# GpSimd splits the row maxima and forms most softmax quotients; the turn stands later

## The chip, the cores and the metric

The kernel runs on one core of one Trainium2 chip. The metric is device microseconds (us) of one execution. The engines are named as in the profile: PE (TensorE, matmuls; PEld are its weight loads), DVE (VectorE), ACT (ScalarE), POOL (GpSimd) and SP (SyncE, which here issues all DMAs). Each engine works through its own instructions in order.

## The reference

Two branches read the same input x of 2048 rows and 512 columns, and a gate mixes them. All data are float32.

```python
g = sigmoid((x * gate_w).sum(-1, keepdims=True))
q, k, v = split(x @ wqkv)                      # 32 heads of 16 columns
scores = q @ k.T * 16 ** -0.5                  # per head
scores = where((i - j >= 0) & (i - j < 256), scores, -1e9)
a = (softmax(scores) @ v) @ wo                 # causal, sliding window of 256
b = gelu(x @ w1 + b1) @ w2 + b2                # 1792 hidden columns
out = g * a + (1 - g) * b
```

## The kernel before, in words

**Precision.** A float32 operand is split into a rounded high part and the rest (type `F32R`), and a dense product is three matmuls (`mm3`, L124 to L129).

**Staging.** A generator (`dense`) yields the dense work: q, k and v for four tiles of 512 rows (PSUM name `qk`, `v`), then eight half MLPs (`u` is x @ w1, `y` is h @ w2), then the output projection (`a`). The attention runs beside it in 128 block steps, 8 head groups of 4 heads times 16 blocks of 128 keys. Each step has four pieces of scores for the maxima (`sm`, `att_max`, L541 on PE, reduced on DVE by L545 into `M`), four pieces of transposed scores (`st`, L585), their exponentials on ACT (L607, into `pt`), and after each fourth block a burst of output matmuls (`att_pvs`, L629, names `pv_sm` and `pv_st`). The maxima run 12 steps ahead of the exponentials (`LEAD`). The span for which there is attention goes from about 120 to 670 us.

**Subtracting the maximum.** The exponential of a transposed score needs the maximum of its query, which lies along the columns there. So the maxima of four blocks (`att_rows`) are split into a high and a low part (`nm`, L557 and L558), turned by a 32 x 32 transpose (L560, `tt`, "the turn"), and written by eight small copies on POOL ("the puts", L567) into the rows of `qs` that stand beside the q stack. The k stack `ks` has constant rows there (`own`, L103), so that the matmul adds the maxima to the scores.

**Cutting the triangles.** A block's exponentials outside the window are set to zero by POOL's `affine_select` (L601), four instructions for a block, and for each fourth block four for either half. The burst `att_pvs` of blocks 1 to 3 of the four bursts in a group pairs the oldest block with the newest, and begins with the newest block's second half; the group's first burst takes the blocks in their order and needs it last.

**Quotients.** Two head groups after two fill a chunk of 128 output columns; the sums of exponentials come out of the same matmuls. After the second group's burst `nd` (sums and weighted values, L650 on ACT, L653 on DVE) is stored, `att_norm` loads the denominators, forms reciprocals (L671), stores them (L674), loads them back spread over rows with the values (`num`, `rb`, L679), multiplies (L683) and stores the chunk (L686). That is done 16 times, for 4 chunks c and 4 row tiles t. The buffers `nd`, `num` and `rb` share one tag of three.

**What sets the order.** Nothing is scheduled by a tool: each engine's order is the order in which the code emits. A clock of planned nanoseconds (`now`) moves with each emitted matmul, and `after(ns, fn)` puts a piece of work on a list that is emitted when the clock passes its due time. So a constant such as `PUT`, or a pair in `DIVS`, says how long after its cause a piece stands in the instruction streams. The five numbers of a row of `DIVS` are the due times of the reciprocal, its store, the loads, the product and the chunk's store; the second row is for the last chunk.

Of the kernel before, what the change touches and what calls it, by code (L numbers as in the profile page):

```python
# [13 lines left out]
ALU = mybir.AluOpType  # L14
# [7 lines left out]
NC = D // 128  # L22
# [10 lines left out]
def gated_mix(ctx: ExitStack, tc: tile.TileContext, x, wqkv, wo, w1, b1, w2, b2, gate_w, out):  # L33
    nc = tc.nc
# [11 lines left out]
    def f32(ap):  # L46
        return ap.bitcast(F32)

    tt = cp.tile([128, 2 * RB, 32], F32, name="tt")
# [28 lines left out]
    nms = cs.tile([128, 2 * RB, 32], F32R, name="nm")  # L78
# [5 lines left out]
    def tables():  # L84

        nc.gpsimd.memset(mask, 0.0)
        for r in (0, 64):
            nc.gpsimd.affine_select(out=mask[r:r + 64, 0:64], in_=mask[r:r + 64, 0:64], pattern=[[1, 64]],
                                    compare_op=ALU.is_ge, fill=NEG, base=-1, channel_multiplier=-1)
            nc.gpsimd.affine_select(out=mask[r:r + 64, 256:320], in_=mask[r:r + 64, 256:320], pattern=[[-1, 64]],  # L90
                                    compare_op=ALU.is_ge, fill=NEG, base=0, channel_multiplier=1)
        nc.gpsimd.memset(cut, 3e38)
        for r in (0, 64):
            for e in (0, 1):
                v = cut[r:r + 64, e]
                nc.gpsimd.affine_select(out=v, in_=v, pattern=[[1 - 2 * e, 64]], compare_op=ALU.is_ge, fill=0.0,
                                        base=-e, channel_multiplier=2 * e - 1)
        nc.gpsimd.memset(nil, 0.0)
        nc.gpsimd.memset(own, 0.0)
        for s in (0, 1):  # L100
            for k in (0, 1):
                v = own[64 * s:64 * s + 4].rearrange("r (p s) -> r s p", s=2)[:, s]
                nc.gpsimd.affine_select(out=v, in_=v, pattern=[[-2, 2]], compare_op=ALU.not_equal,  # L103
                                        fill=1.0, base=-k, channel_multiplier=1)
        nc.gpsimd.memset(f32(nms), 0.0)
        nc.gpsimd.memset(vbuf[:, :, NB * 68:], 0.0)

# [26 lines left out]
    def after(ns, fn, *args):  # L134
        now[1] += 1
        heapq.heappush(todo, (now[0] + ns, now[1], fn, args))
# [414 lines left out]
    def att_rows(g_, rb):  # L551
        need(("v", NT - 2, NB - 1))

        need(*[("max", g_, rb * RB + b, i) for b in range(RB) for i in range(4)])
        m = Ms.pop((g_, rb))
        nm = nms[:, :, 0:4].rearrange("p b (i k) -> p k b i", k=2)
        nc.vector.tensor_scalar(nm[:, 0], m, -1.0, None, op0=ALU.mult)  # L557
        nc.vector.scalar_tensor_tensor(nm[:, 1], m, -1.0, f32(nm[:, 0]), op0=ALU.mult, op1=ALU.subtract)  # L558

        nc.vector.transpose(tt.rearrange("p b c -> p (b c)"), f32(nms).rearrange("p b c -> p (b c)"))  # L560

        def put(i, hb):
            r = 64 * (1 ^ hb ^ i // 2)
            dst = qs[r:r + 4, :, rb * RB * 128:(rb + 1) * RB * 128]
            dst = dst.rearrange("r s (b h i j) -> r s b h i j", b=RB, h=2, i=2)[:, :, :, hb, i % 2]
            src = tt[32 * i:32 * i + 4].rearrange("r (b h) j -> r b h j", h=2)[:, :, hb]
            nc.gpsimd.tensor_copy(dst, src.unsqueeze(1).broadcast_to([4, 2, RB, 32]))  # L567
            if i == 3 and hb:
                done.add(("rows", g_, rb))
        for i in range(4):  # L570
            for hb in range(2):
                after(PUT * (i + 1 + 0.5 * hb), put, i, hb)

    def att_exp(g_, kb, i):

# [87 lines left out]
    def att_norm(t, c):  # L663

        v = ND[t][c].rearrange("g (i r) c -> (g i) r c", r=32)
        den = sb.tile([128, 32], F32, tag="den", bufs=1, name=f"den{t}_{c}")
        nc.sync.dma_start(den, v[:, 16, :].rearrange("i (j c) -> i j c", c=32))
        tiles = []

        def rcp():  # L670
            nc.vector.reciprocal(den, den)  # L671

        def keep():
            nc.sync.dma_start(RD[t][c].rearrange("h (j c) -> (h j) c", c=32), den)  # L674

        def back():
            for name, src in (("num", v[:, 0:16, :]), ("rb", RD[t][c].unsqueeze(1).broadcast_to([8, 16, T]))):
                tiles.append(sb.tile([128, T], F32, tag="tmp", bufs=3, name=f"{name}{t}_{c}"))
                nc.sync.dma_start(tiles[-1], src)  # L679

        def mul():
            num, rb = tiles
            nc.vector.tensor_mul(num, num, rb)  # L683

        def store():
            nc.sync.dma_start(OT[t][c], tiles[0])  # L686
            after(REACH, done.add, ("o", t, c))
        for ns, fn in zip(DIVS[c == NC - 1], (rcp, keep, back, mul, store)):
            after(ns, fn)
# [276 lines left out]
    for u in range(-LEAD, NU):  # L966
        m = u + LEAD
# [51 lines left out]
PUT = 1200  # L1019
# [14 lines left out]
HOLD = 4000.0  # L1034
HOLDQ = 1500.0
HOLDO = 3000.0
DIVS = ((8000, 10000, 16000, 23000, 25000), (4500, 5700, 8500, 17000, 18500))
REST = 1000.0
MXAT = 5500.0
AHEAD = 9e3  # L1040
STEP0 = 2750.0
PVAT = 2
HELD = 2
YAT = 5
YGAP = 2500
# [21 lines left out]
```

## Time and profile before

| | |
|---|---|
| median of 3 runs | 717.82 us (714.51 to 720.12) |
| the profiled execution's own time | 720.44 us |
| its span, first to last instruction | 718.6 us |
| mean granted TensorE clock | 0.994 |
| PE busy | 696.9 us, 97% |
| DVE busy | 514.2 us, 72% |
| ACT busy | 420.0 us, 58% |
| POOL busy | 363.5 us, 51% |
| packets of the DMA queue | 85.9% of 16 engines' span |

A busy time is the sum of an engine's instructions in the one profiled execution. Times in the views count from the start of the span, so they lack the 1.8 us that lie around it. A row of the grouped view reads: line, engine, operation, output and inputs, shape, count, then total busy us and mean ns of one, then how long the engine stood idle just before such instructions and who ended that. A row of the waits reads: who waited for whom, us in total, times, longest. A row of the timeline reads: start, duration, engine, line, operation, count, and in brackets the idle time before it and its releaser. A row of one line's own view gives the shortest, median and longest duration in ns.

### The profile page before, as it was taken

To read this page: it belongs to the slowest core of one execution; us is meant where nothing else is said; L and a number is where in the kernel's file an instruction comes from. 1 tells how busy PE (TensorE), PEld (TensorE's weight loads), DVE (VectorE), ACT (ScalarE), POOL (GpSimd) and SP (SyncE) were. 2 spreads that over 40 slices of the span, in tenths; PEclk is the share of its full clock that TensorE was granted. 3 is DMA by queue.
4 is the path that set the end of the run, shared out by engine and by line. 5 is a ranking of instruction groups with operands and counts; after the bars stand their busy time and mean duration, and the time that the engine had idled before them with its cause. 6 is when DMAs were issued, how large, how long until landed. Compare 5 with 4: busy or idle time off the path is not lost.

```text
span 718.6 us, 17501 instructions
## 1 busy us (share of the span) xinstructions
PE 696.9 (97%) x6129; PEld 599.8 (83%) x6129; DVE 514.2 (72%) x1561; ACT 420.0 (58%) x972; POOL 363.5 (51%) x852
## 2 busy tenths in 40 slices
PE   9999999988999999999999999999999999999998
PEld 7888888776888888888888878888888888868877
DVE  3732425778868977987898789868877986875552
ACT  4434532348546944964696469548845953885451
POOL 4200000548766875786687657757765785620000
PEclk9999999999999999999999999999999999999999
DMA  8989898998998698799776989997799899578573
GB/s 296 355 264 408 286 400 252 286 329 199 276 261 194 149 261 218 192 221 273 187 186 162 243 219 234 236 273 175 187 267 231 211 263 248 137 214 224 191 254 118
DMA packets 179255, 172.09 MB, mean 239 GB/s; under 512 B 56672, under 2 KB 122976, under 8 KB 179168
## 3 DMA queue, kind: packets, MB, share of 16 engines
q1 hardware_dynamic: 179168, 170.97, 85.9%
q8 instruction: 49, 0.80, 0.5%
q14 instruction: 38, 0.31, 0.2%
HBM read 108.53 MB, written 62.39 MB: 238 GB/s over the span
## 4 chain that ended last, share of the span: by engine, by line
PE 76%; DMA 9%; DVE 6%; ACT 6%; issue 1%; SPq 1%; POOL 1%; DVEq 0%; ACTq 0%
PE sm L541 8%; PE st L585 7%; PE pv_sm L629 7%; PE y L127 6%; PE y L129 6%; PE y L128 6%; PE u L127 5%; PE u L129 4%; PE u L128 4%; PE qk L127 3%; PE qk L129 3%; PE qk L128 3%; DMA qd<-SQ 2%; DVE sm L545 2%; DMA raw_w<-in_B_w_dram 2%; PE pv_st L629 2%
## 5 line engine op out<-in xcount | busy, mean ns | idle before, releaser
L545 DVE CUSTOM_DVE_ANT_1 sm<-sm,mask 128x320 f32<-128x320 f32 (+4 forms) x512 | 233.0, 485 | 71.1 <-PE sm L541 66.0
L601 POOL TENSOR_SCALAR_AFFINE_SELECT pt<-pt 64x256 f32<-64x256 f32 (+1 forms) x538 | 215.0, 420 | 102.4 <-ACT pt L607 91.8
L607 ACT ACTIVATE pt<-st 128x320 f32<-128x320 f32 (+4 forms) x512 | 195.4, 422 | 118.2 <-PE st L585 117.4
L541 PE MATMUL sm<-kd,qd 96*128 96x320 f32 (+4 forms) x512 | 148.6, 304 | 8.4 <-DVE M L545 5.1
L585 PE MATMUL st<-qs,ks 128*128 128x320 f32 (+4 forms) x512 | 148.0, 300 | 2.6 <-ACT pt L607 2.5
L567 POOL CAST qs<-tt 4x256 fp32r<-4x256 f32 x256 | 120.2, 470 | 42.7 <-DVE tt L560 31.4
L541 PEld LDWEIGHTS sm<-kd,qd 96*128 96x128 f32 x512 | 97.4, 190 | 28.0 <-DVE M L545 11.7
L585 PEld LDWEIGHTS st<-qs,ks 128*128 128x128 f32 x512 | 98.1, 192 | 14.6 <-ACT pt L607 4.5
L127 PE MATMUL y<-w,h 128*128 128x512 f32 x224 | 85.1, 380 | 0.6 <-DVE sqh L746 0.6
L129 PE MATMUL y<-w,h 128*128 128x512 f32 x224 | 84.9, 379 | 0.0
L128 PE MATMUL y<-w,h 128*128 128x512 f32 x224 | 84.8, 379 | 0.0
L127 PE MATMUL u<-mx,w 128*128 128x512 f32 x196 | 77.4, 395 | 1.2 <-DVE sqh L746 1.2
L129 PE MATMUL u<-mx,w 128*128 128x512 f32 x196 | 74.8, 382 | 0.0
L128 PE MATMUL u<-mx,w 128*128 128x512 f32 x196 | 74.7, 381 | 0.0
L629 PE MATMUL pv_sm<-pt,vbuf 64*32 64x320 f32 (+4 forms) x1408 | 73.2, 346 | 0.2 <-POOL pt L601 0.2
L629 PE MATMUL pv_st<-pt,vbuf 64*32 64x320 f32 (+4 forms) x1408 | 72.9, 346 | 0.0
L545 DVE DVE_READ_ACCUMULATOR2_ANT M<- 128x1 f32 x512 | 71.4, 139 | 0.0
L629 PEld LDWEIGHTS pv_sm<-pt,vbuf 64*32 64x32 f32 x1408 | 49.3, 106 | 20.2 <-issue 2.0
L344 DVE TENSOR_TENSOR qke<-qk,qke 128x512 fp32r<-128x512 f32 x32 | 22.1, 689 | 43.2 <-ACT qke L341 33.9
L341 ACT ACTIVATE qke<-qk 128x512 fp32r<-128x512 f32 x32 | 19.1, 597 | 49.9 <-PE qk L129 34.8
L129 PEld LDWEIGHTS y<-w,h 128*128 128x128 f32 x224 | 42.2, 189 | 6.1
L127 PEld LDWEIGHTS y<-w,h 128*128 128x128 f32 x224 | 42.5, 190 | 3.2 <-DVE sqh L746 0.8
(148 smaller groups left out, 1292.0 us busy)
## 6 DMA issues: line engine op xcount, KB each, us to landing
kd<-SK SPq DMA_DIRECT2D x32, 384.0 KB
qs<-SQ SPq DMA_DIRECT2D x64, 192.0 KB
mx<-XT SPq DMA_DIRECT2D x24, 512.0 KB
SQ<-qke SPq DMA_DIRECT2D x16, 512.0 KB
SK<-qke SPq DMA_DIRECT2D x16, 512.0 KB
ND<-nd SPq DMA_DIRECT2D x32, 256.0 KB
raw_w<-in_B_w_dram SPq DMA_DIRECT2D x28, 256.0 KB
qd<-SQ SPq DMA_DIRECT2D x32, 192.0 KB
```

Source lines behind the costliest of these rows:

```text
L127: nc.tensor.matmul(p, lh, rh, start=first, stop=False)
L128: nc.tensor.matmul(p, lh, rl, start=False, stop=False)
L129: nc.tensor.matmul(p, ll, rh, start=False, stop=last)
L341: nc.scalar.activation(halves(e[:, h]), p, AF.Copy)
L344: nc.vector.tensor_sub(halves(e[:, 1 - h]), p, halves(f32(e[:, h])))
L541: nc.tensor.matmul(v, qd[0:96, n, pr, 128 * j:128 * (j + 1)], two(kd[0:96, n, pr, k1 - w:k1]), start=True, stop=True)
L545: nc.vector.tensor_tensor_reduce(v, v, two(mask[:, 320 - w:320]), 1.0, -3e38, ALU.add, ALU.max, M[:, 2 * (b % RB) + hb, pr:pr + 1])
L567: nc.gpsimd.tensor_copy(dst, src.unsqueeze(1).broadcast_to([4, 2, RB, 32]))
L585: nc.tensor.matmul(pairs(p[:, :w]), ks[:, slot(g_, kb // NB), pr, at:at + 128], two(qs[:, pr, k0:k0 + w]), start=True, stop=True)
L601: nc.gpsimd.affine_select(out=v, in_=v, pattern=[[0, v.shape[1]], [1 - 2 * e, 64]], compare_op=ALU.is_ge, fill=0.0, base=-e, channel_multi ...
L607: nc.scalar.activation(halves(pt[:, hf, pr, :w]), sorted_(p[:, :w]), AF.Exp, scale=SCALE)
L629: nc.tensor.matmul(pv[r // 64][32 * i:32 * i + 32, q - c * T:e - c * T], vts[g_, b // NB][r:r + 64, v:v + 32], rhs(r), start=start, stop=s ...
```

## The change

- The split of the maxima moves from DVE to POOL. POOL copies the maximum into its rounded part and subtracts that; the sign that DVE put on is now in the constant rows of the k stacks, which hold -1 in place of 1.
- The turn on DVE is due 3000 ns after the split (`TURN`) where it followed at once, and the eight puts keep their distance from the turn.
- The product `num * rb` moves from DVE to POOL for the first three chunks (12 of 16); the last chunk's four stay.
- For those twelve the product is due 2000 ns later and the chunk's store 3000 ns later.

```diff
-                                        fill=1.0, base=-k, channel_multiplier=1)
+                                        fill=-1.0, base=-k, channel_multiplier=1)
...
         nm = nms[:, :, 0:4].rearrange("p b (i k) -> p k b i", k=2)
-        nc.vector.tensor_scalar(nm[:, 0], m, -1.0, None, op0=ALU.mult)
-        nc.vector.scalar_tensor_tensor(nm[:, 1], m, -1.0, f32(nm[:, 0]), op0=ALU.mult, op1=ALU.subtract)
-
-        nc.vector.transpose(tt.rearrange("p b c -> p (b c)"), f32(nms).rearrange("p b c -> p (b c)"))
+        nc.gpsimd.tensor_copy(nm[:, 0], m)
+        nc.gpsimd.tensor_sub(nm[:, 1], m, f32(nm[:, 0]))
+
+        def turn():
+            nc.vector.transpose(tt.rearrange("p b c -> p (b c)"), f32(nms).rearrange("p b c -> p (b c)"))
+        after(TURN, turn)
...
-                after(PUT * (i + 1 + 0.5 * hb), put, i, hb)
+                after(TURN + PUT * (i + 1 + 0.5 * hb), put, i, hb)
...
         def mul():
             num, rb = tiles
-            nc.vector.tensor_mul(num, num, rb)
+            (nc.vector if c == NC - 1 else nc.gpsimd).tensor_mul(num, num, rb)
...
-DIVS = ((8000, 10000, 16000, 23000, 25000), (4500, 5700, 8500, 17000, 18500))
+DIVS = ((8000, 10000, 16000, 25000, 28000), (4500, 5700, 8500, 17000, 18500))
...
+TURN = 3000
```

The orders of PE and ACT are the same in both kernels. On SP only the twelve stores of chunks stand later, behind one or two more stores. DVE and POOL change throughout; three places follow, in the rows that the built programs print (line, operation, output and inputs, shape; lines after 560 are one to three higher in the changed kernel).

DVE at the turn for blocks 4 to 7 of the first head group, while the last q and k tiles are made (`sm` is a piece of scores, `M` the maxima, `qke` the split q or k). Before:

```order
L545 ISA sm_8_0_1564,M_8_1561<-sm_8_0_1564,mask 128x320
L557 TENSOR_SCALAR nm<-M_4_1395 128x8x2
L558 SCALAR_TENSOR_TENSOR nm<-M_4_1395,nm 128x8x2
L560 STREAM_TRANSPOSE tt<-nm 128x256
L344 TENSOR_TENSOR qke_3_1575<-qk_3_1538,qke_3_1575 128x512
L545 ISA sm_8_3_1586,M_8_1561<-sm_8_3_1586,mask 128x320
```

Now:

```order
L545 ISA sm_8_0_1564,M_8_1561<-sm_8_0_1564,mask 128x320
L344 TENSOR_TENSOR qke_3_1574<-qk_3_1538,qke_3_1574 128x512
L545 ISA sm_8_3_1585,M_8_1561<-sm_8_3_1585,mask 128x320
L545 ISA sm_8_2_1588,M_8_1561<-sm_8_2_1588,mask 128x320
L545 ISA sm_9_1_1602,M_8_1561<-sm_9_1_1602,mask 128x320
L545 ISA sm_9_0_1604,M_8_1561<-sm_9_0_1604,mask 128x320
L561 STREAM_TRANSPOSE tt<-nm 128x256
```

The split is gone from DVE and the turn stands four maxima further back.

DVE at the product of chunk 1, tile 1, while half an MLP is worked (`u`, `sqh`, `x1h` and `h` are the steps of a GELU, `w` a split weight). Before:

```order
L653 TENSOR_TENSOR nd_3_6000<-nd_3_6000,pv_3_sm 128x512
L545 ISA sm_12_2_6007,M_12_5909<-sm_12_2_6007,mask 128x320
L758 TENSOR_TENSOR h_7_5878<-x1h_7_5878_5885,h_7_5878 128x512
L545 ISA sm_13_1_6032,M_12_5909<-sm_13_1_6032,mask 128x320
L683 TENSOR_TENSOR num_1_5891<-num_1_5891,rb_1_5893 128x512
L746 SCALAR_TENSOR_TENSOR sqh_8_6014_6021<-u_8_5879,x1h_8_6014_6020 128x512
```

Now:

```order
L655 TENSOR_TENSOR nd_3_5996<-nd_3_5996,pv_3_sm 128x512
L545 ISA sm_12_2_6002,M_12_5909<-sm_12_2_6002,mask 128x320
L760 TENSOR_TENSOR h_7_5878<-x1h_7_5878_5885,h_7_5878 128x512
L545 ISA sm_13_1_6027,M_12_5909<-sm_13_1_6027,mask 128x320
L748 SCALAR_TENSOR_TENSOR sqh_8_6009_6016<-u_8_5879,x1h_8_6009_6015 128x512
```

Only the product is missing; what stood behind it follows the maximum at once.

POOL in the third head group's blocks 3 to 7 (`pt` are exponentials; `x4` counts like instructions in a row). Before, with the product of chunk 0, tile 2 on DVE:

```order
L601 AFFINE_SELECT pt_3_3997<-pt_3_3997 64x2x64 x8
L567 CAST qs<-tt 4x2x4x32 x5
L601 AFFINE_SELECT pt_4_4056<-pt_4_4056 64x4x64 x4
L567 CAST qs<-tt 4x2x4x32 x3
L601 AFFINE_SELECT pt_5_4162<-pt_5_4162 64x4x64 x4
L601 AFFINE_SELECT pt_6_4222<-pt_6_4222 64x4x64 x4
L601 AFFINE_SELECT pt_7_4268<-pt_7_4268 64x2x64 x8
```

Now:

```order
L603 AFFINE_SELECT pt_3_3997<-pt_3_3997 64x2x64 x8
L557 CAST nm<-M_12_3763 128x8x2
L558 TENSOR_TENSOR nm<-M_12_3763,nm 128x8x2
L603 AFFINE_SELECT pt_4_4056<-pt_4_4056 64x4x64 x4
L569 CAST qs<-tt 4x2x4x32 x5
L685 TENSOR_TENSOR num_0_4033<-num_0_4033,rb_0_4035 128x512
L569 CAST qs<-tt 4x2x4x32
L603 AFFINE_SELECT pt_5_4157<-pt_5_4157 64x4x64 x4
L569 CAST qs<-tt 4x2x4x32 x2
L603 AFFINE_SELECT pt_6_4219<-pt_6_4219 64x4x64 x4
L603 AFFINE_SELECT pt_7_4268<-pt_7_4268 64x2x64 x8
```

Two small operations stand before block 4's cuts, all eight puts and the product behind them, and two of the puts behind block 5's as well.

## The prediction

> **What bounds the kernel now.** I read the page's busy times first, then the waits of the matrix engine, then the grouped lines of the operations the diff names, and last the timeline at three places.
>
> ```profile
> PE 696.9 (97%) x6129; PEld 599.8 (83%) x6129; DVE 514.2 (72%) x1561; ACT 420.0 (58%) x972; POOL 363.5 (51%) x852
> ...
> PE sm L541 <- DVE M L545: 5.1, 8, 1.0
> PE st L585 <- ACT pt L607: 2.5, 3, 1.5
> PE u L127 <- DVE sqh L746: 1.2, 1, 1.2
> PE pv_sm L629 <- POOL pt L601: 0.2, 1, 0.2
> ```
>
> PE is busy for 696.9 of 718.6 us, so everything that anybody can win back is in the other 21.7 us. DVE costs PE some 6 us of waits in all, POOL 0.2 us. The change lightens DVE and loads POOL, so the question is whether the 6 us shrink by more than the 0.2 us grow.
>
> ```profile
> L557 DVE TENSOR_SCALAR nm<-M 128x16 fp32r<-128x16 f32 x32 | 7.9, 247 | 0.0
> L558 DVE SCALAR_TENSOR_TENSOR nm<-M,nm 128x16 fp32r<-128x16 f32 x32 | 5.8, 182 | 1.1
> L683 DVE TENSOR_TENSOR num<-num,rb 128x512 f32<-128x512 f32 x16 | 11.9, 746 | 1.5 <-DMA rb<-RD 1.5
> L201 POOL TENSOR_TENSOR w<-raw_w,w 128x512 fp32r<-128x512 f32 x11 | 14.3, 1304 | 28.5 <-ACT w L197 24.0 <-PE qk L129 4.3
> L213 POOL CAST qk<-raw_qk 128x512 fp32r<-128x512 f32 x1 | 0.6, 612 | 4.0 <-DMA raw_qk<-in_A_wqkv_dram 4.0
> ```
>
> **What DVE loses.** The two split operations go, 7.9 + 5.8 = 13.7 us in 32 places, and twelve of the sixteen products, 12 x 0.746 = 9.0 us, with the 1.5 us for which one of them waited: 24 us of DVE's 514. Where DVE keeps up, which is nearly everywhere, that is worth nothing; PE covers it. It is worth something at three places.
>
> ```profile
> 415.12 0.59 SPq L679 DMA_DIRECT2D rb<-RD  x1
> ...
> 423.66 0.90 DVE L683 TENSOR_TENSOR num<-num,rb 128x512 f32<-128x512 f32 x1 [1.55 <-DMA rb<-RD]
> ...
> 425.21 0.48 PE L127 MATMUL u<-mx,w 128*128 128x512 f32 x1 [1.17 <-DVE sqh L746]
> ...
> 422.00:427.30 5.30, 3.86 (x19) 2.78 (x18) 3.75 (x13) 3.69 (x9) 2.89 (x8) 1.00 0.77 165
> 427.30:430.70 3.40, 3.40 (x12) 2.86 (x11) 3.22 (x10) 2.28 (x6) 0.97 (x2) 0.50 0.96 236
> 157.50:161.00 3.50, 3.50 (x11) 3.10 (x12) 2.57 (x9) 2.80 (x7) 2.20 (x3) 0.52 1.05 383
> 171.00:174.00 3.00, 1.44 (x7) 1.01 (x8) 2.65 (x4) 2.97 (x7) 2.83 (x5) 1.00 0.41 83
> ```
>
> At 422 us DVE stands 1.55 us before a product whose reciprocals were asked for at 415.12 and arrive only 8.5 us later; the GELU step behind it is late and PE idles 5.30 - 3.86 = 1.44 us (a window's row gives its length, the busy time of PE, its weight loads, DVE, ACT and POOL, then the granted clock). In the next 3.40 us the clock is granted at 0.50, which costs another 1.70 us. The changed kernel has this product on POOL and asks for it 9 us after the load where it was 7, so DVE passes. The 1.44 us go. Whether the slow stretch goes with them is open: it follows the stall, but between 171 and 174 us PE idled 1.56 us and the clock stayed at 1.00. I take half, 0.85. Term A: 1.44 + 0.85 = 2.3 us, between 1.4 and 3.1.
>
> [...]
>
> ```profile
> 442.46 0.89 DVE L683 TENSOR_TENSOR num<-num,rb 128x512 f32<-128x512 f32 x1
> ...
> 440.90:451.00 10.10, 9.35 (x48) 7.37 (x47) 10.10 (x33) 8.73 (x21) 7.92 (x17) 1.00 1.02 248
> ...
> 142.54 1.27 POOL L201 TENSOR_TENSOR w<-raw_w,w 128x512 fp32r<-128x512 f32 x1 [4.27 <-PE qk L129]
> 142.62 1.22 DVE L557 TENSOR_SCALAR nm<-M 128x16 fp32r<-128x16 f32 x1
> 145.70 0.40 PE L541 MATMUL sm<-kd,qd 96*128 96x320 f32 x1 [0.81 <-DVE M L545]
> ```
>
> From 440.9 to 451 us DVE is busy throughout and PE short of 10.10 - 9.35 = 0.75 us; the 0.89 us product lies in that stretch and goes. Term B: 0.75 us. At 142.62 the split took 1.22 us in place of its 0.25, ending as POOL's 1.27 us product ended (143.84 and 143.81), and PE then waited 0.81 us for the maxima. There the change takes the split off DVE and puts the turn (0.45 us) behind four more maxima. Term C: 0.81 us. Together A + B + C = 3.9 us, between 3.0 and 4.7.
>
> **What POOL gains.** Twelve products at the 1.27 us of the unhindered row: 15.3 us. The split's two operations are in no row of POOL; they lie between nothing and the 0.61 us cast of L213, which moves 32 times as much. I take 0.2 and 0.25 us, 14 us in 32 places. Busy time is no price, however: POOL runs in order, and PE's output matmuls (L629) for blocks 1 to 3 of a head group begin with the very last triangles (L601) that POOL has cut. So what counts is how late the last cut is. Here is the stretch in which the changed POOL order was shown, with the score row that PE reaches at its end.
>
> ```profile
> 303.98 1.14 POOL L601 TENSOR_SCALAR_AFFINE_SELECT pt<-pt 64x128 f32<-64x128 f32 x4
> 305.17 3.06 POOL L567 CAST qs<-tt 4x256 fp32r<-4x256 f32 x5
> 308.27 2.04 POOL L601 TENSOR_SCALAR_AFFINE_SELECT pt<-pt 64x256 f32<-64x256 f32 x4
> 310.26 1.74 POOL L567 CAST qs<-tt 4x256 fp32r<-4x256 f32 x3
> 312.06 1.97 POOL L601 TENSOR_SCALAR_AFFINE_SELECT pt<-pt 64x256 f32<-64x256 f32 x4
> 314.54 3.58 POOL L601 TENSOR_SCALAR_AFFINE_SELECT pt<-pt 64x256 f32<-64x256 f32 x8 [0.51 <-ACT pt L607]
> 318.77 1.14 POOL L601 TENSOR_SCALAR_AFFINE_SELECT pt<-pt 64x128 f32<-64x128 f32 x4 [0.64 <-ACT pt L607]
> ...
> 307.41 0.43 ACT L607 ACTIVATE pt<-st 128x320 f32<-128x320 f32 x1
> ...
> 320.00 0.24 PE L629 MATMUL pv_sm<-pt,vbuf 64*32 64x64 f32 x1
> ```
>
> Before, five puts (L567) fill POOL's time from 305.17 to 308.23, while ACT has no exponentials ready; the last cut ends at 319.91, 0.09 us ahead of PE. Afterwards the turn comes some 3 us later and all eight puts stand behind the cuts of block 4, which can start when their exponentials end, at 307.84. From there POOL has 2.04 + 3.06 + 1.74 + 1.97 + 3.58 + 1.14 = 13.53 us of the same work and 1.27 us of product: it ends at 322.6, 2.6 us after PE wants it. That is the upper end. The lower end is nothing: eight puts at the short end of their row (0.39 us) and twelve cuts at 0.41 and eight at 0.29 make 10.4 us, with the product 11.6, done at 319.5. The rows hold 3.1 us of stretching by DVE, and I have no reason to expect it gone, only some of it.
>
> ```profile
> 564.90 2.87 POOL L567 CAST qs<-tt 4x256 fp32r<-4x256 f32 x5
> 567.82 2.47 POOL L601 TENSOR_SCALAR_AFFINE_SELECT pt<-pt 64x256 f32<-64x256 f32 x4
> 570.24 1.27 POOL L567 CAST qs<-tt 4x256 fp32r<-4x256 f32 x3
> 571.58 2.12 POOL L601 TENSOR_SCALAR_AFFINE_SELECT pt<-pt 64x256 f32<-64x256 f32 x4
> 574.59 5.21 POOL L601 TENSOR_SCALAR_AFFINE_SELECT pt<-pt 64x256 f32<-64x256 f32 x12 [0.89 <-ACT pt L607]
> ...
> 566.88 0.43 ACT L607 ACTIVATE pt<-st 128x320 f32<-128x320 f32 x1
> ...
> 579.13 0.24 PE L629 MATMUL pv_sm<-pt,vbuf 64*32 64x64 f32 x1
> L567 POOL CAST qs<-tt x256: 388/396/927, 129.1 to 633.8; 4x256 fp32r<-4x256 f32 x128
> L601 POOL TENSOR_SCALAR_AFFINE_SELECT pt<-pt x538: 286/409/971, 162.8 to 627.1; 64x256 f32<-64x256 f32 x112, 64x128 f32<-64x128 f32 x68
> ```
>
> The same stretch four head groups later: 567.31 + 13.94 + 1.27 = 582.5, against 579.80 before: up to 2.7 us more. The other stretches have no product behind block 4 or more slack; I allow six of them the 0.5 us of the split, 3.0 us at most. Term D: between 0 and 2.6 + 2.7 + 3.0 = 8.3 us; I take the middle, 4.2, since the hindered durations are what the rows show and the product's place is certain, but PE's own lateness gives POOL some of it back.
>
> **Edits at nothing.** The sign moves into a constant written once. The turn and the puts, 3 us later: even by the upper sum the last put ends at 322.6 - 3.58 - 1.14 = 317.9, and the first score matmul reads its rows seven block steps after the maxima, each of (318.77 - 303.98) / 4 = 3.7 us, at about 303.98 + 25.9 = 329.9; 12 us of cover are left. DVE's turn waits for POOL's split, and behind it would queue the maxima and then PE: POOL needs the 1.14 us of cuts at 303.98 and 0.45 us for the split, 1.6 of the 3 us that the plan gives it. The store of the products moves 3 us back and past two stores on SP's queue; its readers come at the end of the kernel. ACT's copy of the sums (L650) gains a wait for the product that read its buffer, one period old by then.
>
> **The sum.** The profiled execution took 720.44 us, 2.6 above the median of 717.82. On it: 720.4 - 3.9 + 4.2 = 720.7. Carried to the median that is 718.1; but the late reciprocals of term A may be what made this execution slow, and then its 2.3 us aren't there to win. I add half of them: 719.3 us, which is no change; about 1%, 7 us, is what a measurement tells from none.
>
> **Rivals.** *POOL keeps ahead* (D is nothing): 717.8 - 4.7 = 713.1 us. For it: POOL is busy only 51% and its wait list is all ACT; against it, the 0.09 us of slack above. *POOL becomes the path*: D at 8.3, with the clock halved after the two stalls of over 2 us as after 422, 2 x 1.7, and only B and C won: 717.8 - 1.6 + 8.3 + 3.4 = 727.9 us. It decides where the last cut ends over 2 us behind PE. *The lock*: a POOL product holds up DVE operations with two inputs for up to 1.27 us, as the split at 142.62 was held. The four products of one head group pair, two of which are the rows at 423.66 and 442.46, stand where DVE is bound: 4 x 1.27 = 5.1 us of PE, in place of A and B: 717.8 - 0.8 + 4.2 + 5.1 = 726.3 us. For it the split's row, against it that DVE has slack elsewhere. *DVE was the hidden brake*: all DVE waits of PE vanish with both halved-clock stretches (the other is the row at 157.50): 6.3 + 3.4 = 9.7 us, 708.1 us; against it, that DVE is busy for only 72% of the span. *Nothing moves off the path*, since the turn still stands on DVE and waits for POOL: 717.8 us, part of my forecast.
>
> [...]
>
> **Chances.** Forecast (713.5 to 724.5) 0.50; POOL ahead 0.20; POOL the path 0.14; the lock 0.06; the brake 0.10. Faster by over 1% (below 710.6) is the brake and a little of POOL ahead: 0.12. Slower by over 1% (above 725.0): POOL the path, most of the lock: 0.18. The range reaches from the brake's edge to the path's: 709 to 729.
>
> **What would show it.** Right: no DVE wait for reciprocals, DVE some 22 us less busy, POOL 25 to 30 us busier, and a PE wait for POOL cuts of several us where 0.2 stood, in the stretches that end near 320 and 579 us. Wrong: those waits absent, or PE waits on DVE unchanged or longer, or a DVE wait for the split.

## The result, and the profile after

The changed kernel takes 728.04 us (median of six runs, 724.31 to 729.51), the kernel before 718.94 us (six runs beside them, 714.51 to 722.42). The ratio is 1.0107, 95% interval 1.0076 to 1.0139: slower by 1%, 9.1 us. The time lies inside the range on record, 8.7 us above the forecast, and within 0.2 us of the rival "POOL becomes the path" (727.9). The profiled execution took 729.51 us, with a span of 727.8.

The busy times of the page, after:

```profile
PE 702.4 (97%) x6129; PEld 603.6 (83%) x6129; DVE 500.2 (69%) x1485; ACT 419.7 (58%) x972; POOL 391.0 (54%) x928
```

POOL is 27.5 us busier, DVE 14.0 us less busy, and neither number tells where 9 us went: both engines are far from full. PE's waits (line, what it waited for, us in total, times, longest) do:

```profile
PE sm L541 <- DVE M L545: 4.0, 7, 1.2
PE pv_st L631 <- POOL pt L603: 3.6, 3, 2.1
...
PE pv_sm L631 <- POOL pt L603: 1.7, 5, 0.7
```

(Lines from 574 on stand two further down than in the kernel before.) The waits for maxima fell from 5.1 to 4.0 us; the waits of the output matmuls for POOL's cuts rose from 0.2 to 5.3 us. The groups of the new work on POOL:

```profile
L685 POOL TENSOR_TENSOR num<-num,rb 128x512 f32<-128x512 f32 x12 | 16.9, 1410 | 1.0
L558 POOL TENSOR_TENSOR nm<-M,nm 128x16 fp32r<-128x16 f32 x32 | 8.4, 263 | 2.7
L557 POOL CAST nm<-M 128x16 fp32r<-128x16 f32 x32 | 7.6, 236 | 1.9 <-DVE M L545 0.2
```

A product takes 1.41 us on average (1.27 at the least, 1.79 at the most), the split's two steps 0.24 and 0.26 us. POOL's timeline in the stretch of which the prediction showed the rows of before:

```profile
305.82 0.20 POOL L557 CAST nm<-M 128x16 fp32r<-128x16 f32 x1
306.10 0.22 POOL L558 TENSOR_TENSOR nm<-M,nm 128x16 fp32r<-128x16 f32 x1
307.08 2.07 POOL L603 TENSOR_SCALAR_AFFINE_SELECT pt<-pt 64x256 f32<-64x256 f32 x4 [0.76 <-ACT pt L609]
309.20 2.14 POOL L569 CAST qs<-tt 4x256 fp32r<-4x256 f32 x5
311.42 1.66 POOL L685 TENSOR_TENSOR num<-num,rb 128x512 f32<-128x512 f32 x1
313.15 0.39 POOL L569 CAST qs<-tt 4x256 fp32r<-4x256 f32 x1
313.60 2.06 POOL L603 TENSOR_SCALAR_AFFINE_SELECT pt<-pt 64x256 f32<-64x256 f32 x4
315.72 1.17 POOL L569 CAST qs<-tt 4x256 fp32r<-4x256 f32 x2
316.95 4.42 POOL L603 TENSOR_SCALAR_AFFINE_SELECT pt<-pt 64x256 f32<-64x256 f32 x12
```

From 307.08 to the last cut's end at 321.37 no row but the first has an idle time in brackets: all eight puts and the product stand between cuts that the output matmuls wait for. Before, five of the puts stood ahead of the first cut, and the last two rows each began with 0.5 and 0.6 us of waiting for ACT. PE at that place:

```profile
319.00 0.30 PE L631 MATMUL pv_sm<-pt,vbuf 64*32 64x64 f32 x2
320.59 0.30 PE L631 MATMUL pv_st<-pt,vbuf 64*32 64x64 f32 x4 [1.29 <-POOL pt L603]
...
324.97 0.27 PE L631 MATMUL pv_sm<-pt,vbuf 64*32 64x128 f32 x1
```

The burst of 96 output matmuls takes 5.97 us from its first start to its last, where an undisturbed one takes 2.13 (1.71 for the bursts of 72). PE is idle for 1.6 us of the 3.84 more. Most of the rest shows in the windows around this burst and the one near 584 us (length, busy us of PE, weight loads, DVE, ACT, POOL, then the granted clock):

```profile
319.00:321.20 2.20, 0.62 (x11) 0.30 (x10) 0.53 (x2) 0.44 (x1) 1.99 (x9) 1.00 0.96 284
321.20:324.60 3.40, 3.40 (x74) 2.71 (x82) 0.45 (x1) 0.00 (x0) 0.60 (x3) 0.51 1.12 252
...
584.00:587.20 3.20, 0.86 (x17) 0.36 (x23) 1.72 (x6) 1.38 (x3) 2.99 (x9) 1.00 0.91 267
587.20:590.60 3.40, 3.40 (x77) 2.73 (x85) 0.45 (x1) 0.00 (x0) 0.54 (x3) 0.55 1.13 235
```

Behind both stalls the clock is granted at 0.51 and 0.55 for 3.4 us: 3.40 x 0.49 + 3.40 x 0.45 = 3.2 us more.

How much longer than undisturbed each burst is, in the profiled executions of the two kernels and of the experiments below (us; one execution each, places are approximate, nothing under 0.2 listed):

| kernel | where, and how much | sum |
|---|---|---|
| before | 579: 0.46 | 0.5 |
| changed | 304: 0.24, 319: 3.84, 389: 0.32, 456: 1.26, 521: 1.13, 569: 0.29, 584: 4.58, 636: 0.56 | 12.2 |
| E1 due times, E3 and E9 products on POOL, E10 | none | 0 |
| E2 split on POOL, late turn | 320: 1.15, 388: 0.32, 521: 1.11, 584: 1.78, 633: 0.45 | 4.8 |
| E6 late turn alone | 325: 1.20, 393: 0.30, 525: 1.26, 588: 0.77, 637: 0.55 | 4.1 |
| E7 split on POOL, turn at once | 178: 0.65, 586: 0.89 | 1.5 |
| E4, E12 split and products on POOL, turn at once | 177: 1.20, 321: 1.13, 455: 0.28, 582: 1.28 (E12: 0.65, 1.11, none, 1.29) | 3.9, 3.1 |
| E5 changed, three products back | 180: 1.00, 308: 0.24, 324: 0.72, 391: 0.31, 523: 1.11, 571: 0.28, 586: 1.26, 635: 0.55 | 5.5 |
| E8 changed, earlier products | 319: 0.67, 386: 0.32, 519: 1.11, 582: 0.83, 630: 0.54 | 3.5 |
| E11 changed, split back on DVE | 320: 2.14, 388: 0.30, 437: 0.48, 518: 1.28, 567: 0.29, 582: 1.90, 632: 0.55 | 6.9 |

The two profiled spans differ by 9.2 us. The bursts make +11.8 of it, the stretch between the bursts at 417 and 437 us -1.4 (19.85 before, 18.46 after, from first matmul to first matmul), the part ahead of the first burst -1.3, and the rest +0.1.

### The profile page after: what moved, and what is told of

It is laid out like the page before. It is cut to its first block, busy times and chain, and to the rows that moved or that the text cites. A ratio compares the mean times of both kernels' runs of the same rounds, so it can differ in the third digit from the quotient of the medians.

```text
span 727.8 us, 17505 instructions
## 1 busy us (share of the span) xinstructions
PE 702.4 (97%) x6129; PEld 603.6 (83%) x6129; DVE 500.2 (69%) x1485; ACT 419.7 (58%) x972; POOL 391.0 (54%) x928
## 4 chain that ended last, share of the span: by engine, by line
PE 69%; DMA 8%; POOL 8%; ACT 6%; DVE 5%; issue 2%; SPq 1%; POOLq 0%; DVEq 0%; ACTq 0%
PE pv_sm L631 8%; PE sm L541 7%; PE st L587 6%; POOL pt L603 6%; PE y L127 6%; PE y L129 6%; PE y L128 6%; PE u L127 3%; PE qk L127 3%; PE qk L129 3%; PE qk L128 3%; DMA raw_w<-in_B_w_dram 3%; PE u L128 3%; PE u L129 3%; DMA kd<-SK 2%
## 5 line engine op out<-in xcount | busy, mean ns | idle before, releaser
L569 POOL CAST qs<-tt 4x256 fp32r<-4x256 f32 x256 | 112.4, 439 | 43.8 <-DVE tt L561 32.6
L587 PEld LDWEIGHTS st<-qs,ks 128*128 128x128 f32 x512 | 97.7, 191 | 14.8 <-ACT pt L609 4.8
L631 PE MATMUL pv_st<-pt,vbuf 64*32 64x320 f32 (+4 forms) x1408 | 78.3, 358 | 3.6 <-POOL pt L603 3.6
L631 PE MATMUL pv_sm<-pt,vbuf 64*32 64x320 f32 (+4 forms) x1408 | 78.7, 358 | 1.8 <-POOL pt L603 1.7
L631 PEld LDWEIGHTS pv_sm<-pt,vbuf 64*32 64x32 f32 x1408 | 53.6, 109 | 22.5 <-issue 3.9
L631 PEld LDWEIGHTS pv_st<-pt,vbuf 64*32 64x32 f32 x1408 | 49.4, 109 | 4.3 <-POOL pt L603 4.1
L652 ACT ACTIVATE nd<-pv_st 128x512 f32<-128x512 f32 x32 | 19.1, 598 | 56.9 <-PE pv_sm L631 44.7
```

What stands on the lines that cost most here:

```text
L587: nc.tensor.matmul(pairs(p[:, :w]), ks[:, slot(g_, kb // NB), pr, at:at + 128], two(qs[:, pr, k0:k0 + w]), start=True, stop=True)
L631: nc.tensor.matmul(pv[r // 64][32 * i:32 * i + 32, q - c * T:e - c * T], vts[g_, b // NB][r:r + 64, v:v + 32], rhs(r), start=start, stop=s ...
```

## The experiments

The change has three separable parts: the split on POOL, the turn 3 us later, the products on POOL. All ratios are against the kernel before, run on the same chip beside the experiment, with 95% intervals. Each experiment that is based on the changed kernel has its sign in the constants. The due times differ too, and it matters below: in the changed kernel, E1, E3 to E5 and E9 to E12 the product is due 9 us after the load of its reciprocals (25000 - 16000 ns). In E2, E6 and E7 it is due after 7 us as in the kernel before, since their edits take `DIVS` back as well, although the expectations of all three speak of the changed due times. In E8 it is 7 us, with both earlier.

**E1, the due times alone** (kernel before):

```diff
-DIVS = ((8000, 10000, 16000, 23000, 25000), (4500, ...
+DIVS = ((8000, 10000, 16000, 25000, 28000), (4500, ...
```

> The kernel before with only the later due times of the changed kernel (product 25 us after the load of the sums, store 28), all products still on DVE, split and turn as before. Reciprocals theory (my term A): DVE no longer stands 1.55 us at the product near 422 us, PE does not stall there and the clock is not halved behind it; the time is 1 to 3 us below the kernel before, a ratio of 0.996 to 0.999. Rival: the stall at 422 us is a rare event of one execution, or another late DMA takes its place; ratio 1.000, with a half-clock stretch of 3.4 us still near 425 to 435 us.

718.31 us, 0.9989 (0.9958 to 1.0019): by the time alone the reciprocals theory and its rival can't be told apart. The profile is for the theory. The same product starts 9.85 us after its load, without a wait,

```profile
413.75 0.59 SPq L679 DMA_DIRECT2D rb<-RD  x1
...
423.60 0.92 DVE L683 TENSOR_TENSOR num<-num,rb 128x512 f32<-128x512 f32 x1
```

and no clock is halved until the matmuls end. From the burst near 417 us to that near 437 this kernel takes 18.0 us where the kernel before took 19.8. The gain is lost again behind it: to the next burst it takes 18.6 us instead of 17.3, and from the burst near 577 to the next 17.5 instead of 16.5, where DVE waits 0.87 us for the reciprocals of another product. Why the first of these two stretches is longer isn't shown.

**E2, the changed kernel with the products back on DVE, at the due times of the kernel before:**

```diff
-            (nc.vector if c == NC - 1 else nc.gpsimd).tensor_mul(num, num, rb)
+            nc.vector.tensor_mul(num, num, rb)
...
-DIVS = ((8000, 10000, 16000, 25000, 28000), (4500, ...
+DIVS = ((8000, 10000, 16000, 23000, 25000), (4500, ...
```

> The changed kernel with the twelve products back on DVE, at the changed due times: only the split is on POOL and the turn 3 us later. Chain theory (POOL's work between the first cuts of a block row and the output matmuls is the path, late puts and product add up in it, and a stall over 2 us halves the clock for 3.4 us): without its 1.7 us product the chain is late by 2.37 - 1.7 = 0.7 us at the burst near 319 us and 3.14 - 1.7 = 1.4 us near 584 us, neither halves the clock; time 719 to 722 us, ratio 1.001 to 1.005. Rival, split and turn cost it all: 726 us or more, with the half-clock stretches behind both bursts. Rival, the products cost it all: 716 to 718 us, last cuts no later than before.

723.98 us, 1.0052 (1.0021 to 1.0083), as the chain theory has it. The late cuts are 1.36 and 1.99 us behind PE (0.7 and 1.4 expected), and no clock is halved there. The 2 us of the expectation were an estimate: in the changed kernel the clock was granted at 0.51 and 0.55 behind cuts 2.37 and 3.14 us late, in the kernel before at 1.00 where PE idled 1.56 us between 171 and 174 us. They are no rule: the 1.44 us ahead of 427 us in the kernel before were followed by half clock, and a stall of 3.0 us in E8 was not. POOL's timeline shows why the split isn't what costs:

```profile
306.56 0.20 POOL L557 CAST nm<-M 128x16 fp32r<-128x16 f32 x1
306.84 0.22 POOL L558 TENSOR_TENSOR nm<-M,nm 128x16 fp32r<-128x16 f32 x1
308.36 2.07 POOL L603 TENSOR_SCALAR_AFFINE_SELECT pt<-pt 64x256 f32<-64x256 f32 x4 [1.29 <-ACT pt L609]
310.47 3.50 POOL L569 CAST qs<-tt 4x256 fp32r<-4x256 f32 x6
```

POOL does the split and then stands 1.29 us before the first cuts. What is missing there are the puts, which before filled this time and now come after the cuts. And DVE, which does the products in this run, 7 us after the load as in the kernel before:

```profile
417.99 0.59 SPq L681 DMA_DIRECT2D rb<-RD  x1
...
427.59 0.84 DVE L685 TENSOR_TENSOR num<-num,rb 128x512 f32<-128x512 f32 x1 [3.00 <-DMA rb<-RD]
```

It stands 3.00 us for the reciprocals, longer than before, and starts 9.60 us after the load. At this product it is 2.13 us in E6 and 3.30 in E7, with the same due times. The kernels side by side, by how long after the load this product is due, with the time from the burst near 417 us to that near 437:

| due, engine | kernels and time, us |
|---|---|
| 7 us, DVE | before 19.8, E2 21.1, E6 20.0, E7 21.9 |
| 7 us, POOL | E8 19.9 |
| 9 us, DVE | E1 18.0 |
| 9 us, POOL | changed 18.5, E3 18.4, E4 17.9, E5 19.2, E9 18.0, E10 18.6, E11 17.5, E12 17.7 |

The clock is halved in this stretch in the four kernels of the first row and in no other. So what removes the stall is the later due time; E1 shows that it does so with the product still on DVE. Since E2, E6 and E7 have no run with the later due times, what the late reciprocals cost in their times isn't separated.

**E3, the products alone on POOL** (kernel before, with the due times of E1):

```diff
-            nc.vector.tensor_mul(num, num, rb)
+            (nc.vector if c == NC - 1 else nc.gpsimd).tensor_mul(num, num, rb)
```

> The kernel before with the twelve products on POOL at the changed due times; split on DVE and turn as before. Chain theory: the chain was 0.09 us ahead near 320 us and 0.68 late near 579; with 1.7 us of product it is late by 1.6 and 2.4 us, so only the second halves the clock: 1.6 + 1.7 + 1.7 + some 1 us elsewhere, less the 1 to 3 us won by the due times: 720 to 724 us, ratio 1.002 to 1.007. Rival, the products cost it all: 726 us or more. Rival, the split and turn cost it all: 716 to 718 us.

718.85 us, 0.9981 (0.9955 to 1.0007): less than the chain theory's 720 to 724, and the rival of the products falls. POOL's timeline of the fullest stretch:

```profile
307.44 2.11 POOL L601 TENSOR_SCALAR_AFFINE_SELECT pt<-pt 64x256 f32<-64x256 f32 x4
309.51 1.27 POOL L567 CAST qs<-tt 4x256 fp32r<-4x256 f32 x3
310.86 1.28 POOL L683 TENSOR_TENSOR num<-num,rb 128x512 f32<-128x512 f32 x1
312.09 5.70 POOL L601 TENSOR_SCALAR_AFFINE_SELECT pt<-pt 64x256 f32<-64x256 f32 x12
318.19 1.14 POOL L601 TENSOR_SCALAR_AFFINE_SELECT pt<-pt 64x128 f32<-64x128 f32 x4 [0.40 <-ACT pt L607]
```

The last cut ends 0.03 us after PE wants it (before: 0.09 us ahead). Before, POOL waited 0.51 and 0.64 us for ACT between these cuts, and its three puts took 1.74 us where they now take 1.27: the product fits into what was idle time and hindrance. With the puts ahead of the first cuts, the product is free.

It gains nothing that these runs can tell, though DVE has 9 us less to do. In the stretch from which term B was to come, POOL's product holds up DVE (timeline of E3, rows of three engines):

```profile
445.13 1.27 POOL L683 TENSOR_TENSOR num<-num,rb 128x512 f32<-128x512 f32 x1
...
445.25 1.69 DVE L201 TENSOR_TENSOR w<-raw_w,w 128x512 fp32r<-128x512 f32 x1 [0.76 <-ACT w L197]
...
447.47 0.40 PE L541 MATMUL sm<-kd,qd 96*128 96x320 f32 x1 [1.47 <-DVE M L545]
```

DVE's step of the weight split (L201), 0.82 us on average before, begins 0.12 us after POOL's product and takes 1.69 us; the maxima queue behind it and PE waits 1.47 us. E9 shows the same at 446.60 us (1.80 us, PE waits 1.56). But this is little of the reason: from the burst near 437 us to the next E3 and E9 take 18.9 us, and E1, with the product on DVE, takes 18.6 where the kernel before took 17.3.

**E4, the changed kernel with the turn at once:**

```diff
-TURN = 3000
+TURN = 0
```

> The changed kernel with the turn asked for right behind the split again (0 in place of 3 us), split and products on POOL. Chain theory: POOL's chain holds the same work, only its 0.76 us idle before the first cuts is filled by puts; the bursts near 319 and 584 us stay 1.6 and 2.4 us late: 724 to 728 us, and DVE waits for POOL's split rise from 10.6 us to over 30 us in all. Rival, the late puts are the cost: 716 to 720 us. Rival, DVE's wait for the split is the cost: 732 us or more, with PE's waits for maxima over 10 us where they are 4.0.

726.99 us, 1.0092 (1.0056 to 1.0127). The waits of DVE's turn for POOL's split rise, to a little less than expected:

```profile
DVE tt L561 <- POOL nm L558: 27.4, 22, 3.2
```

but PE's waits for maxima are 5.2 us against 5.8 in E1: DVE's wait is mostly covered. The last cuts are 1.34 and 1.50 us behind PE (1.6 and 2.4 expected). The profiled execution (723.41 us) was the fastest of its six; its bursts account for 3.9 us.

**E5, the changed kernel with the products of tile 2 on DVE:**

```diff
-            (nc.vector if c == NC - 1 else nc.gpsimd).tensor_mul(num, num, rb)
+            (nc.vector if c == NC - 1 or t == 2 else nc.gpsimd).tensor_mul(num, num, rb)
```

> The changed kernel with the products of tile 2 only (three of the twelve, those at 311, 444 and 577 us) back on DVE; the other nine stay on POOL. Full-stage theory (POOL is full only in the stage of tile 2, where its chain of cuts, puts and product has no idle left; elsewhere idle time takes the products): the bursts near 319 and 584 us are stretched by 1.2 and 1.8 us as with no product on POOL at all, in place of 3.8 and 4.6, no clock halved behind them; time as with the split alone, 722 to 725 us, ratio 1.003 to 1.007. Rival, each product costs its share wherever it stands: three of twelve give back a quarter of the 4 us between the changed kernel and the split alone: 727 us, ratio 1.009 or more.

725.58 us, 1.0072 (1.0042 to 1.0101). The bursts near 324 and 586 us are stretched by 0.72 and 1.26 us, less than expected, at full clock, and the one near 457 is not stretched. Three of twelve products bring the ratio from 1.0107 to 1.0072, a third of the whole change, but it lies just above what the theory wanted and the interval reaches to the rival's 1.009. The profile is for the theory, the time alone doesn't decide.

**E6, the late turn alone** (the changed kernel with split and products on DVE, at the due times of the kernel before):

```diff
-        nc.gpsimd.tensor_copy(nm[:, 0], m)
-        nc.gpsimd.tensor_sub(nm[:, 1], m, f32(nm[:, 0]))
+        nc.vector.tensor_copy(nm[:, 0], m)
+        nc.vector.tensor_sub(nm[:, 1], m, f32(nm[:, 0]))
...
-            (nc.vector if c == NC - 1 else nc.gpsimd).tensor_mul(num, num, rb)
+            nc.vector.tensor_mul(num, num, rb)
...
-DIVS = ((8000, 10000, 16000, 25000, 28000), (4500, ...
+DIVS = ((8000, 10000, 16000, 23000, 25000), (4500, ...
```

> Split back on DVE, products on DVE, the turn 3 us later as in the changed kernel (the sign in the constants, due times of the changed kernel). Late-puts theory (in the run with the split on POOL, POOL did the split and then still stood 1.29 us idle before the first cuts, so the split cost nothing there; what costs is that all puts come behind the first cuts): bursts near 320 and 580 us stretched by 1.1 and 1.8 us all the same, time 722 to 725 us, ratio 1.003 to 1.007. Rival, the split's POOL time is the cost and the turn's place costs nothing: bursts 2.1 us long, 717 to 719 us, ratio 0.996 to 1.000.

725.67 us, 1.0055 (1.0027 to 1.0084), the late-puts theory's ratio and not the rival's. POOL here has not one instruction more than before, and is late all the same:

```profile
313.37 2.06 POOL L603 TENSOR_SCALAR_AFFINE_SELECT pt<-pt 64x256 f32<-64x256 f32 x4 [2.37 <-ACT pt L609]
315.47 3.49 POOL L569 CAST qs<-tt 4x256 fp32r<-4x256 f32 x6
```

It idles 2.37 us ahead of the first cuts and does the puts behind them. The profiled execution (729.86 us) was the slowest of its twelve, and 5.0 of the 9.2 us that its span is longer than before lie ahead of the first burst, where PE waits up to 3.2 us for a load and the clock is halved for 6.8 us; the bursts make 3.6 of it, which is about what the median shows (4 us).

**E7, the split on POOL with the turn at once, products on DVE** (E2 with the diff of E4):

> Split on POOL, products on DVE, the turn asked for right behind the split as in the kernel before (TURN 0, due times of the changed kernel). Late-puts theory: the puts may again fill POOL's time before the first cuts, but come behind the split, which waits for the cuts of the block row before; chain late by about 0.2 to 0.5 us near 320 us (1.4 with product, less 1.3), DVE waits for the split some 30 us, hidden for the most part: 718 to 721 us, ratio 0.998 to 1.002. Rival, DVE's wait for POOL's split costs by itself: 724 us or more, with PE's waits for maxima above 8 us (4.7 to 5.9 in the other runs).

725.48 us, 1.0052 (1.0024 to 1.0080): a miss of both, since the time is the rival's and its sign in PE's waits is absent. The puts are where the theory put them, behind the split and ahead of the first cuts,

```profile
309.62 3.05 POOL L569 CAST qs<-tt 4x256 fp32r<-4x256 f32 x5 [0.54 <-DVE tt L561]
```

and the burst at 323 us isn't stretched; those at 178 and 586 us are, by 1.5 us together. PE's waits for maxima are 6.3 us, not above 8. In the profiled execution the largest loss is elsewhere: DVE waits 3.3 us for reciprocals, at the due time of the kernel before, PE 2.7 us behind it, and at least 5.5 us at half clock follow. That stretch is 2.1 us longer than in the kernel before. Whether its other runs lose the same there isn't shown.

**E8, the changed kernel with the product 4 us earlier:**

```diff
-DIVS = ((8000, 10000, 16000, 25000, 28000), (4500, ...
+DIVS = ((8000, 10000, 14000, 21000, 28000), (4500, ...
```

> The changed kernel with the product due 21 us after the load of the sums in place of 25, and the reciprocals asked for at 14 in place of 16: the product then stands right behind the split, ahead of the first cuts of the block row, where POOL was idle 0.76 to 4.4 us. Full-stage theory: near 319 us 0.8 to 1.3 us of the product's 1.28 go into that idle time, the last cut is 1.4 to 1.9 us late in place of 2.4, and the clock is halved at one burst at most: 722 to 726 us, ratio 1.003 to 1.008. Rival, the cost is POOL's whole load wherever the product stands: 727 to 729 us. Risk in both: the reciprocals took 8.5 us once and have 7 here, POOL would wait 1.5 us for them.

725.06 us, 1.0063 (1.0032 to 1.0095), within the theory's range. The product now fills the idle time ahead of the first cuts, which is gone from brackets:

```profile
306.04 1.27 POOL L685 TENSOR_TENSOR num<-num,rb 128x512 f32<-128x512 f32 x1
307.43 2.06 POOL L603 TENSOR_SCALAR_AFFINE_SELECT pt<-pt 64x256 f32<-64x256 f32 x4
```

The burst behind it is 0.67 us longer instead of 3.84. POOL waits 5.0 us in all for reciprocals, with the product due 7 us after their load where the changed kernel has 9 and no such wait.

**E9, E3 once more, and E10, all sixteen products on POOL** (E3, and `nc.gpsimd.tensor_mul(num, num, rb)` without the condition):

> Once more the kernel before with only the twelve products on POOL at the changed due times, split and turn as before. Idle-time theory (with the puts ahead of the first cuts POOL waits 1.2 us for exponentials in the fullest stage and the product goes into that wait; DVE no longer stands for late reciprocals): no output burst stretched, no stall of PE near 422 us, 0 to 3 us below the kernel before, ratio 0.996 to 1.000, and with the first measurement of 0.998 clear of 1 if it is real. Rival: the product on POOL gains nothing, ratio 0.999 to 1.002.

> As the kernel with the twelve products alone on POOL, with the last four products on POOL too, where POOL has no cuts left to do. Idle-time theory: POOL's product takes 1.28 us in place of DVE's 0.68, 0.6 us more before each store of products that the output projection reads; DVE's own work there gets 0.68 us lighter each time: within 1 us of the kernel with twelve, ratio 0.996 to 1.001. Rival: the output projection waits for each of the four, 4 x 0.6 = 2.4 us, ratio 1.001 to 1.004.

718.98 us, 1.0008 (0.9983 to 1.0032), and 718.35 us, 1.0003 (0.9971 to 1.0034). With E3's 0.998 that is no difference: the products alone on POOL neither cost nor gain, twelve or sixteen.

**E11, the changed kernel with the split alone back on DVE** (the first diff of E6):

> The changed kernel with the split alone back on DVE: products on POOL, turn 3 us late. Late-puts theory (POOL's split falls into idle time before the first cuts and costs nothing; late puts and product add up): the bursts near 320 and 584 us as in the changed kernel, stretched by 2 to 4.6 us, half clock behind at least one, ratio 1.008 to 1.012. Rival, the split's 16 us on POOL are a good part of the cost: bursts stretched by 1 to 2 us, no half clock, ratio 1.003 to 1.006.

728.67 us, 1.0130 (1.0099 to 1.0161): the changed kernel's loss in full without the split. The chain is packed in the same way,

```profile
307.82 2.07 POOL L603 TENSOR_SCALAR_AFFINE_SELECT pt<-pt 64x256 f32<-64x256 f32 x4 [1.33 <-ACT pt L609]
309.93 2.13 POOL L569 CAST qs<-tt 4x256 fp32r<-4x256 f32 x5
312.15 1.68 POOL L685 TENSOR_TENSOR num<-num,rb 128x512 f32<-128x512 f32 x1
```

the last cuts are 2.36 and 2.58 us behind PE, and the bursts are stretched by 2.14 and 1.90 us. In one point the expectation failed: no clock was halved behind them in this execution.

**E12, E4 once more:**

> Once more the changed kernel with the turn right behind the split, for a second profiled execution (the first was the fastest of its six, 3.6 us under their median, and showed 3.9 us of stretched bursts). Late-cut theory: bursts again stretched by 3 to 5 us near 178, 321, 455 and 582 us, and the rest of the time in a clock halved somewhere: ratio 1.005 to 1.010. Rival, DVE's wait for the split (27 us in all) costs PE more than the first profile showed: PE's waits for maxima 7 us or more in place of 5.2.

724.80 us, 1.0072 (1.0039 to 1.0104). PE's waits for maxima are 6.0 us and the bursts 3.1 us longer, as the late-cut theory has it; a wait of 2.5 us of PE for DVE in the output projection is the largest single one.

Side by side, the ratios of the eight kernels:

| | products on DVE | products on POOL |
|---|---|---|
| split on DVE, turn at once | 1 (before), 0.9989 (E1) | 0.9981, 1.0008 (E3, E9) |
| split on POOL, turn at once | 1.0052 (E7) | 1.0092, 1.0072 (E4, E12) |
| split on DVE, late turn | 1.0055 (E6) | 1.0130 (E11) |
| split on POOL, late turn | 1.0052 (E2) | 1.0107 (changed) |

The left column is at the due times of the kernel before, except for E1, and the right one at those of the changed kernel; by E1 that difference alone is nothing that these runs can tell. The late turn alone costs 0.6%. The split on POOL with the turn at once costs 0.5% beside products on DVE (E7, with the late reciprocals in its profile) and 0.6 to 1.1% beside products on POOL (E4 and E12 against E3 and E9), and nothing once the turn is late (compare the last two rows). The products cost nothing by themselves and another 0.6 to 0.8% with the late turn: the idle time that would have taken them is spent. None of the kernels beats the kernel before by what these runs can tell.

## Why the prediction was right in its range and low in its number

**What bounds the kernel** held: PE's waits decided, not busy times.

**DVE's side.** Term A, 2.3 us (1.4 to 3.1), measured 1.4: the wait for reciprocals and the half clock are gone, but between 431.25 and 432.66 us PE now stands 1.1 us for exponentials. Of the two reasons given, the later due time is the one that E1 shows to suffice; the other engine isn't needed for it. The open half, whether the slow stretch goes with the stall, went its way: the clock is not halved there in any kernel that is due 9 us after the load. Term B, 0.75 us, came to nothing: from the burst at 437 to that at 454 us the two executions take 17.3 and 17.4 us. Term C, 0.81 us, was won, and by the late turn, not by the split's engine: PE's stall near 146 us is absent with the late turn (E2, E5, E6, E8, changed; 0.35 us in E11) and there in every kernel with the turn at once (0.7 to 1.2 us in E1, E3, E4, E7, E9, E10, E12).

**Term D, the step that failed.** The mechanism was right, at the two places and in the order of rows that it named; the size was not. It gave 0 to 8.3 us and took 4.2. The stretching by DVE that its upper end holds is in the trace of the kernel before: the 186 puts with DVE busy for at least half of their time took 0.50 us on average, the 49 with DVE busy for under 5% of it 0.39. The bursts grew by 11.8 us in the profiled execution. The half clock behind two of them, which the forecast left to a rival, makes 3.2 of that; without it 8.6 remain, just above the upper end. The chain near 320 us was put between 11.6 and 14.8 us long and took 14.3. The reason for the middle, that PE's own lateness would give POOL time back, finds nothing in the runs: PE reached the burst at 319.00 us, 1.0 us earlier than before, and waited there. What I should have read from my own rows is that the one idle stretch ahead of the first cuts, where the five puts stood, would be lost, and that no other was left between these cuts. Of the six other stretches, costed at 0.5 us each for the split, it is not the split that is late (E11) but the puts again.

**Edits at nothing.** "The turn and the puts, 3 us later" looked at who reads the puts, and no score matmul did wait for them. But the price is paid by what queues behind them on POOL. I had it in D only together with the products; E6 shows it as a cost by itself, 0.6%, half of the whole. DVE's wait for the split (10.6 us in all) stayed covered, as stated.

**The rivals.** "POOL becomes the path" is what happened, with its condition: last cuts 2.37 and 3.14 us behind PE, the clock halved after both, 727.9 us against 728.0. That the two agree within 0.2 us is in part luck: it started from 717.8 us where the kernel before took 718.9 beside the changed one, and it counted on term B, which didn't come, and not on A, which did. It had a chance of 0.14, and with the upper end of D as the likelier one it should have been the forecast. "The lock" stalls PE at one place: a DVE operation of 0.8 us takes 1.7 to 1.8 beside a POOL product in E3 and E9, and PE waits 1.5 us, not 5.1; in the changed kernel the long ones are POOL's own products, up to 1.79 us. The row that the prediction rests it on, L557 at 142.62, has one input and not two. One with two is in the same trace: DVE's part of the weight split (L201) at 171.35 us takes 1.74 us, beside 0.70 in the median, begins 0.08 us after POOL's 1.27 us part of it and ends 0.55 us after that does. The row at 445.25 in E3 is alike: DVE's step begins 0.12 us after POOL's product and ends 0.54 us after it. Not every neighbour is hit: the 25 full maxima (128 x 320) that overlap one of the changed kernel's twelve products take 0.51 us on average, and so do all 448. "POOL keeps ahead" is what E3 and E9 show for the products alone.

**What would show it.** A POOL wait of PE of several us (5.3 in all, 3.9 of it in the stretches that end near 320 and 584), no DVE wait for reciprocals and POOL 27.5 us busier: right. DVE "some 22 us less busy": the groups that went made 22.9 us, its busy time fell by 14.0; neighbouring rows of DVE overlap, and busy time counts the overlap once (its rows add up to 634.8 us before and 615.1 after, its busy time is 514.2 and 500.2). One sign of being wrong came too, a DVE wait for the split (10.6 us in 9 places), but PE's waits for maxima fell all the same.

**What stays open.** Why the split on POOL with the turn at once costs 0.5% and more is known in part: stretched bursts explain 1.5 us of it in E7 and 3 to 4 in E4 and E12. Two stretches are longer than before in all three: from the end of the first burst to the next (15.9 us instead of 15.0, with waits for maxima of 0.54 and 0.42 us), and behind the fifth (14.4 instead of 13.8). The late reciprocals of E7 are another part in one execution. Open is also how often the clock is halved in a run: the six runs of the changed kernel were granted 0.993 to 1.000 on average, and the one at 1.000 was the fastest, 724.31 us, the one at 0.993 the slowest.

## What to carry to other kernels

An engine that is busy for half of the span can be full in one stage: add new work to the queue between the moment when its input is there and the moment when the next engine wants its output, and count the idle time in that stretch alone. A filler that is moved later costs nothing by its own reader and can still cost everything that queues behind it; look first at which idle time it used to fill. Two edits that each fit the same idle time must be priced together.

## What the runs showed of the hardware

**The same stall may or may not halve the clock.** Windows of the changed kernel:

```profile
154.03:157.44 3.41, 0.43 (x3) 0.47 (x4) 0.82 (x4) 0.00 (x0) 0.00 (x0) 1.00 1.07 312
157.44:160.85 3.41, 3.41 (x11) 2.89 (x10) 2.33 (x8) 3.26 (x7) 2.14 (x3) 0.50 1.05 387
```

and of E8 at the same place of the program:

```profile
152.72:156.13 3.41, 2.17 (x11) 1.60 (x9) 2.70 (x8) 1.59 (x3) 1.01 (x1) 1.00 1.02 252
156.13:159.54 3.41, 1.70 (x10) 1.65 (x11) 0.92 (x3) 1.09 (x3) 0.39 (x1) 1.00 0.99 361
159.55:162.96 3.41, 3.41 (x21) 3.09 (x19) 3.19 (x9) 3.38 (x8) 1.85 (x4) 1.00 1.02 329
```

PE's longest wait there is about 3 us both times (3.2 and 3.0), and half clock follows after one only. Before, 1.44 us of idling ahead of 427 us had been enough. What differs is where the stall lies on a grid. In the changed kernel's execution the half-clock stretches begin, as long as matmuls run, at 157.44, 321.28 and 587.52 us, 163.84 and 266.24 us apart: 48 and 78 times 3.413 us, and each is 3.41 us long. E8's only one begins at 719.33 us, behind the last matmul, and lies on such a grid with the windows shown. In the changed kernel one grid window holds 2.98 us of PE's idling; in E8 the stall is split over two, with 1.24 and 1.71 us. On the grids of the kernel before and the changed one, as long as matmuls run, half clock follows the five windows in which PE idles longest: 2.13 and 1.44 us before (windows from 154.26 and 423.91 us), 2.98, 1.58 and 2.34 us in the changed kernel (from 154.03, 317.87 and 584.11 us). It follows no other; the longest idling in these is 1.31 us before (from 686.74) and 1.11 us in the changed kernel (from 430.51). Why E8's 1.71 us had no half clock behind it isn't shown. A stall thus has two prices, its idle time and, where half clock follows, 3.41 x 0.50 = 1.7 us more; a forecast needs both.
